# New fixed orders for all five engines of an adaLN block with linear attention and a SiLU MLP, up to the MLP's second unit

## The chip, the cores and the metric

The kernel runs on one core of a Trainium2 chip. A core has five engines, each with an instruction queue of its own that is worked off strictly in order: TensorE (PE in the profile; its weight loads are shown as PEld), VectorE (DVE), ScalarE (ACT), GpSimd (POOL) and SyncE (SP), which here only issues DMAs. Engines wait for each other through semaphores. The metric is the device time of one execution in microseconds, the median of several runs. The kernel before takes 1138.91 us (three runs, 1138.76 to 1139.21).

## The reference

Input x has 2048 tokens of 576 values. A conditioning vector gives six vectors of 576 (shifts, scales and gates). Then come linear attention with 32 heads of 18 values and an MLP with 4608 hidden values, each behind a LayerNorm and each added back with its gate.

```python
mod = (_silu(c) @ w_mod).reshape(c.shape[0], 6, 1, -1)
sa, ca, ga, sb, cb, gb = (mod[:, 0], mod[:, 1], mod[:, 2], mod[:, 3], mod[:, 4], mod[:, 5])
h = _layernorm(x, axis=-1) * (1 + ca) + sa
x = x + ga * _A_ref(h, A_wqkv, A_wo)
h = _layernorm(x, axis=-1) * (1 + cb) + sb
x = x + gb * _B_ref(h, B_w1, B_w2)
...
phi = lambda t: jnp.where(t > 0, t + 1, jnp.exp(t)) + 1e-6
pq, pk = phi(q), phi(k)
kv = jnp.einsum("bhsd,bhse->bhde", pk, v)
z = jnp.einsum("bhsd->bhd", pk)
num = jnp.einsum("bhqd,bhde->bhqe", pq, kv)
den = jnp.einsum("bhqd,bhd->bhq", pq, z)[..., None] + 1e-6
...
h = jnp.einsum("bsd,df->bsf", x, w1)
h = _silu(h)
out = jnp.einsum("bsf,fd->bsd", h, w2)
```

## The kernel before

Nearly all products are made in three passes over operands split into a rounded high part and a remainder (`x_passes`, L226): high by high, high by low, low by high. So most results cost one ACT operation that rounds (a CAST) and one VectorE subtraction that gives the remainder (`sub_hi`, L121).

The 2048 tokens are 16 tiles of 128, in four blocks of 512. The program goes through these stages:

- The head, up to about 36 us. The modulation columns are summed from `w_mod` (L360, L362, matmuls L371), the first block's x is normalised (L191, L193), turned by TensorE transposes (L390) and modulated (L199, L201), and the key product of the first two tiles is made (L407) while its weights are still being loaded and split (L309, L310, L315, L317; L317 on POOL). `warm_up` (L412) gives PE matmuls whose result nobody reads. A one-column exponential, `warm` (L431), stands in the program right behind the SiLU of the conditioning vector.
- The attention's first part, up to about 200 us: for each tile the key, value and query products (`k_proj`, `v_proj`, `q_proj`; matmuls L226 into the two `psK` tiles, two PSUM banks each), the map phi (L326 the exponential on ACT; L333 and L334 on VectorE), the split of v (L544, L548), the sum of k by v in three banks that stay in use (L589), and the transposes of the next block (L214). `mod_piece` (L517, L519) sums other parts of the modulation on VectorE.
- The turn to the second part, up to about 223 us: the product of kv and the output weights (L777).
- The attention's second part and the first piece of the MLP, up to about 368 us, in banks `big` (three of two banks) and `small` (two): transposes of the normalised q (L812), the attention's output (L226), LayerNorm again, the chunks of the second hidden input (`turn_chunk_k`, L214 into `small`), and the first 256 hidden values of the MLP (L886 up with SiLU L888, L897 down).
- The rest: 17 groups of 256 hidden values, each in two units of 1024 tokens (`do_unit`), with matmuls up (L1324) and down (L1397) by seven products in place of eight. From the third unit on, about 402 us, every engine works in the order of the code (`manual_schedule(engines=ENGINES)`).

Up to the second unit a scheduler sets the order of the engines that aren't in a `manual_schedule` block, and the table `ORDERS` overrides it: `arrange` (from L135 on) takes, engine by engine, the instructions in the order in which the code wrote them, numbers them, and ties each to the one before it in the table, without a semaphore wait of its own. Before, PE was in `manual_schedule` too, and its table row was the code's own order but for two transposes; DVE, ACT, POOL and SP had full tables.

```python
tc.add_manual_dep(i, before.name, no_wait, reason="arrange")
```

Of the kernel before, what the change touches and what calls it, by code (L numbers as in the profile page):

```python
# [2 lines left out]

# [19 lines left out]
def kernel(ctx: ExitStack, tc, A_x, A_wqkv, A_wo, B_x, B_w1, B_w2, c, w_mod, out):  # L23
# [28 lines left out]
    def f32(ap):  # L52
# [1 line left out]

    ORDERS = {
        "PE": """
            0-106 114 107-109 115 110-113 116-2586
        """,
        "DVE": """
            0 3 2 1 4 6-7 11 8 12-13 9-10 14-16 18 17 5 19-22 30 23-24 28-29 25-27 43 31 44 33-34 36 35 37-38 32 39  # L60
            41 40 42 45-47 50 48-49 62-63 51-53 57 84 64 55 58 65 59 86 66 85 87 60 56 80 67 88 81 83 68 82 69 71 70
            72 122 73-74 61 89 54 75 78 76 90 77 79 123 91 124 92-93 96-97 125 98 94 126-127 100 99 95 101 103-104
            107 105 108 106 109 111 102 132-133 135 110 134 136 138-139 137 140-144 112 145 148 113 146 149 147 114
            117 115 118 116 119-121 128-129 131 150-151 225 223 130 226 224 222 152-155 157-158 156 159 162 176 160
            177-178 161 179-181 163 165 228 227 166-167 164 169-170 168 171-173 193-197 199 198 200 202 201 203-205
            174 209 206-207 210 208 175 182 185 183 186 188 187 184 189-190 192 191 211-213 216 214 217 215 218 220
            219 221 229 232 230 233 231 234-237 240 238-239 241-243 246 244 247 245 248-249 252 250-251 253-256 258
            257 259 263 260-262 266 268 267 270 269 271 264-265 272-273 275-277 274 281 279 282 278 280 283-284 288
            285 289 286 295-296 290 306 303 302 291 307 292 314 293 315 294 297 323 304 298-299 324 308 331 287 300
            309 301 310-311 305 312 316 332 340 313 317-319 341 320-321 325 351 322 326-329 352 362 330 333-336 338  # L70
            363 337 339 344 370 345-347 342-343 349 348 353 371 380 354-359 350 360 381 361 398 364-369 399 416
            372-375 377 376 378 417 424 385 382 384 379 387-388 391-392 394 425 402 386 389 403 390 404-407 393 383
            395 413 408 412 409 397 418 396 414 410 415 401 419 411 420-421 423 400 422 427-428 426 429 431-439 430
            440 445 441 446 443 442 444 447-451 455 454 453 452 466 456 467 469 457 464 471 458-460 475 472 462 461
            463 478 473 477 484 483 485-486 479 468 480 474 487 470 465 493 488 495 490 476 489 482 492 481 491 494
            529 500-501 499 497 496 498 510 503 502 511 507 506 504-505 508 515 509 514 527 513 512 518 528 519
            516-517 523 520-522 524-526 531 530 533 532 534-535
        """,
        "Activation": """
            0-2 4-6 9 7-8 10 3 11-12 16 19 13-14 18 17 15 21 26 20 27 22-23 29 24 28 25 30-31 35 32-33 36-37 55 57  # L80
            39 56 40 38 42 41 44 43 58 45 50 53 59 54 34 51-52 60 46 48-49 47 61-62 65 63 66-67 69 68 70 64 71-75
            77-78 76 79 81-82 80 83 93 95 94 84-85 96 87 86 88-91 97 92 99 98 100-102 104-105 103 106 108-109 107
            150 149 110-111 151 112 153 152 113-114 116-117 115 118 120 119 121-122 131 133 123-124 132 134 126 125
            127-130 135 137 136 138-139 141-142 140 145 143 146 144 147-148 154-155 157-158 156 159 161 160 162-182
            184 186 185 183 188 187 189-190 193 191 194-195 192 196-198 200 202 199 201 203-208 212 217 209 214 213
            210 216 211 219 215 224 234 220 218 239 221 225 222-223 235 245 228 230 226 232 256 227 231 229 233
            236-237 240 238 241 243 242 246 249 270 247 244 250-251 248 272 252-253 257 254-255 278 266 264 267 265
            258 261 268-269 262 271 263 260 293 259 273 305 274-276 281 283 282 277 284 279 307 285-287 296 289 280
            288 290 292 291 301 299 297 302 306 303 300 304 294-295 308 298 309-311 313 312 314-317 322-323 321 320
            319 318 324 341 325 339 326 342 327 338 344 328 330 340 332 329 333 331 343 347 336 334 337 335 349 345  # L90
            348 353-354 350 355-356 351 358 352 357 346 359 364-365 363 387 360-361 369 371 368 366 362 374 367 370
            372 376 378 373 384 377 379 375 389 385 381-383 386 380 388 390-395 397 396
        """,
        "Pool": """
            6-7 0 3 8 2 4-5 9-15 20 16-17 19 18 21-27 34 28 31 29 35 30 32-33 38 36 42 37 39 45 48 40 43-44 51 46-47
            41 55 49-50 58 52-53 61 56-57 73 85 54 59-60 77 62-63 80 64 74 65 75 68-69 78 66 72 70 79 76 67 71 81-84
            90-92 95 93 86-88 94 101 89 103 105 99-100 96 106 98 121 97 102 107 123-124 104 108-109 114 111 110
            112-113 115-116 118-120 125 122 117 126-128
        """,
        "SP": """  # L100
            0-25 57 30-31 26 28 27 29 32 39 33-34 54 53 55-56 40-46 35-38 47-52 61 63 60 66 64 58 62 65 59 67 69 68
            70-71 75-76 74 72-73 77-82 85 83 86 84 87-88 95 91 89 92 97 93 90 98 94 96 99-102 104 103 119 106-107
            105 110 117 108 118 112 109 111 113-116 123 120-122
        """,
    }

# [531 lines left out]

    QB = NT // 2
    qs = iter(range(NT))  # L640
    with tc.manual_schedule(engines={mybir.EngineType.PE}):
        for t in range(NT):
            tb, i = t // 4, t % 4
            more = tb + 1 < NB
# [43 lines left out]
            if t == 10:  # L688
                load_wo()

    with tc.manual_schedule(engines={mybir.EngineType.PE}):
        qs = iter(range(QB, NT))
        finish_wo()
        edges_of_wo(range(NHC - 2))
# [524 lines left out]
                lns[tb].normalise(i, xn2[tb][i], acc[4 * tb + i], A if tb < 2 or i in (0, 1) else V)  # L1219


    with tc.manual_schedule(engines={mybir.EngineType.PE}):
# [322 lines left out]

    unit = None
    units = [(g, p) for g in range(1, NG) for p in range(2)]
    with tc.manual_schedule(engines={mybir.EngineType.PE}):
        fetch(5)
        for u in U:  # L1550
            G.memset(u, 0.0)
# [41 lines left out]
```

## Time and profile before

| what | value |
|---|---|
| median of three runs | 1138.91 us |
| the profiled execution, span on the core | 1136.9 us |
| instructions in the profile | 19287 |
| HBM read, written | 250.12 MB, 16.78 MB |
| granted TensorE clock, every slice | 0.9 or more |
| mean DMA rate over the span | 237 GB/s |

The profiled execution has no time of its own beside the span; the 2.0 us between the span and the median lie outside of it. A row of the timeline begins with its start in us from the span's start and its duration; neighbours of one line are merged (x4 is four of them), and brackets give the idle time before it and what ended it. A row of the waits gives the total in us, the count and the longest. A row of the windows gives the length of the stretch and the busy time and count of each engine, then the clock, the DMA share and GB/s.

### The profile page before, as it was taken

What the parts mean: (1) busy time and instruction counts of PE and PEld (TensorE: products, weight loads), DVE (VectorE), ACT (ScalarE), POOL (GpSimd) and SP (SyncE); (2) the same over time, 40 slices, a digit from 0 to 9 for tenths busy, and PEclk for the clock granted to TensorE, in tenths of its full rate; (3) what the DMA queues carried; (4) which work ended last, traced back from release to release, by engine and by line L of the source; (5) the groups of instructions that cost most, each with busy time, mean ns of one, the idle gap of its engine ahead of it and who ended that gap; (6) DMA issues with size and microseconds to landing.
All of it is one profiled execution on the core that took longest, in us unless ns stands there. A gap on an engine that the chain in (4) does not pass through costs nothing.

```text
span 1136.9 us, 19287 instructions
## 1 busy us (share of the span) xinstructions
PE 1126.8 (99%) x7033; PEld 1040.8 (92%) x7033; DVE 971.0 (85%) x1543; ACT 538.7 (47%) x1112; POOL 649.3 (57%) x743
## 2 busy tenths in 40 slices
PE   8999999999999999999999999999999999999998
PEld 7999999999998899999999999999989999999998
DVE  6866744686878899999999999999999999999996
ACT  5643442547556544445445444444444444444441
POOL 1100000374714777767775776677667767776786
PEclk9999999999999999999999999999999999999999
DMA  9621100223359877976978869779778697697684
GB/s 281 199 84 31 44 7 1 71 84 116 137 198 354 340 274 256 348 278 257 361 261 315 314 250 356 273 255 364 261 277 331 265 344 281 258 346 274 256 310 156
DMA packets 58813, 269.03 MB, mean 237 GB/s; under 512 B 5724, under 2 KB 21856, under 8 KB 35680
## 3 DMA queue, kind: packets, MB, share of 16 engines
q1 hardware_dynamic: 58708, 267.80, 64.4%
q8 instruction: 56, 0.92, 0.3%
q14 instruction: 37, 0.30, 0.1%
q10 hardware_dynamic: 12, 0.00, 0.0%
HBM read 250.12 MB, written 16.78 MB: 235 GB/s over the span
## 4 chain that ended last, share of the span: by engine, by line
PE 94%; DMA 3%; DVE 1%; ACT 1%; POOL 0%; SPq 0%; issue 0%; POOLq 0%
PE up L1324 34%; PE down L1397 32%; PE psK L226 12%; PE big L226 7%; PE small L886 2%; PE big L897 2%; PE kvp L589 1%; DMA hT<-in_w_mod_dram 1%; PE big L812 1%; DMA raw<-in_w_mod_dram 1%; DMA hT<-hd 1%; PE small L214 1%; DMA xt<-in_A_x_dram 1%; PE up L1427 1%; PE down L1427 1%; PE psT L214 1%
## 5 line engine op out<-in xcount | busy, mean ns | idle before, releaser
L1405 DVE TENSOR_TENSOR acc<-down,acc 128x576 f32<-128x576 f32 x330 | 246.2, 754 | 13.2 <-PE down L1397 3.2
L1324 PE MATMUL up<-hT,w 128*128 128x512 f32 x916 | 239.4, 390 | 0.5 <-DMA hT<-hd 0.5
L1324 PEld LDWEIGHTS up<-hT,w 128*128 128x128 f32 x916 | 164.5, 188 | 25.4 <-DMA hT<-hd 0.7
L1359 POOL TENSOR_TENSOR s<-f,f 128x256 f32<-128x256 f32 x66 | 52.3, 792 | 159.7 <-ACT f L1340 159.7
L1397 PE MATMUL down<-w,hb 128*128 128x288 f32 x792 | 120.6, 294 | 0.0
L1397 PE MATMUL down<-w,hc 128*128 128x288 f32 x792 | 120.6, 294 | 0.0
L1397 PEld LDWEIGHTS down<-w,hc 128*128 128x128 f32 x792 | 113.7, 188 | 5.4 <-PE up L1324 0.3
L1397 PEld LDWEIGHTS down<-w,hb 128*128 128x128 f32 x792 | 113.7, 188 | 5.3
L121 DVE TENSOR_TENSOR w<-v,w 128x288 fp32r<-128x288 f32 (+1 forms) x170 | 114.8, 684 | 2.8 <-ACT w L1058 2.8
L1405 DVE TENSOR_TENSOR U<-down,U 128x576 f32<-128x576 f32 x132 | 99.6, 754 | 17.1 <-PE down L1397 15.2
L226 PE MATMUL psK<-w,hT 128*128 128x352 f32 (+3 forms) x506 | 106.4, 336 | 1.1 <-POOL w L317 0.6
L1324 PE MATMUL up<-room,w 128*128 128x512 f32 x348 | 91.0, 390 | 0.0
L1378 POOL TENSOR_TENSOR hc<-s,hc 128x512 fp32r<-128x512 f32 x66 | 89.4, 1355 | 0.1
L184 POOL TENSOR_TENSOR rstd<-ve,neghalf 128x4 f32<-128x4 f32 (+3 forms) x10 | 9.5, 953 | 138.8 <-DVE ve L183 138.8
L226 PEld LDWEIGHTS psK<-w,hT 128*128 128x128 f32 x506 | 81.8, 188 | 7.5 <-POOL w L317 0.8
L1340 ACT ACTIVATE f<-f 128x512 f32<-128x512 f32 x102 | 64.5, 632 | 47.8 <-DVE f L1345 24.8
L1343 DVE TENSOR_TENSOR f<-up,p 128x512 f32<-128x512 f32 x102 | 69.7, 683 | 12.1 <-PE up L1324 11.2
L1066 ACT CAST w<-v 128x288 fp32r<-128x288 f32 x85 | 36.7, 434 | 76.4 <-PE down L1397 62.1
L1324 PEld LDWEIGHTS up<-room,w 128*128 128x128 f32 x348 | 62.5, 188 | 9.4
L1363 POOL TENSOR_TENSOR f<-f,s 128x256 f32<-128x256 f32 x66 | 51.2, 776 | 34.9 <-DVE hb L1378 24.5
L1397 PE MATMUL down<-w,he 128*128 128x288 f32 x396 | 63.0, 294 | 0.0
L1397 PE MATMUL down<-w,ha 128*128 128x288 f32 x396 | 63.0, 294 | 0.0
(310 smaller groups left out, 2529.7 us busy)
## 6 DMA issues: line engine op xcount, KB each, us to landing
hT<-hd SPq DMA_DIRECT2D x66, 1280.0 KB, 5.5
hT<-hd SPq DMA_DIRECT2D x45, 1024.0 KB, 5.5
room<-hd SPq DMA_DIRECT2D x35, 1280.0 KB, 5.7
room<-hd SPq DMA_DIRECT2D x20, 1024.0 KB, 5.1
v<-in_B_w_dram SPq DMA_DIRECT2D x17, 576.0 KB, 7.2
v<-in_B_w_dram SPq DMA_DIRECT2D x17, 512.0 KB, 7.1
hd<-S SPq DMA_DIRECT2D x6, 1024.0 KB, 3.8
xt<-in_A_x_dram SPq DMA_DIRECT2D x16, 288.0 KB, 5.2
```

The lines of the kernel that those rows point to most:

```text
L121: return V.tensor_sub(lo, full, f32(hi))
L214: T.transpose(ps[:, i * P : (i + 1) * P], xt[i][:, cidx * P : (cidx + 1) * P], ident)
L226: T.matmul(ps, xpart(a), wpart(b), start=n == 0, stop=n == len(XW) - 1)
L1066: A.copy(self.w2[n][:, 0], src)
L1324: T.matmul(ps, left, right, start=first and m == 0, stop=m == len(seq) - 1, skip_group_check=True)
L1340: A.activation(self.f[i, k], self.f[i, k], AF.Silu)
L1343: V.tensor_add(f, self.bank[bank[1]], self.p1)
L1359: G.tensor_add(self.s[:, 0:1], half(i, 0, 1), half(i, 1, 1))
L1363: G.tensor_sub(half(i, 1, 0), half(i, 1, 0), self.s[:, 1:2])
L1378: eng.tensor_sub(t[:, :, 1, :], src, f32(t[:, :, 0, :]))
L1397: T.matmul(ps[:, p, :HALF], self.a[i, n][:, u, p * P : (p + 1) * P], self.w.w2[n][:, v], start=n in (1, 5, 7, 6) and j == 0, stop=j == 2, ...
L1405: V.tensor_add(dst, ps[:, :, :HALF], dst)
```

## The change

The five tables are replaced and the five `manual_schedule(engines={PE})` blocks become plain blocks, so that PE's order comes from its table alone. The numbers in the tables stand for the same instructions as before. Lines after the table are 82 further down in the changed file.

```diff
     ORDERS = {
         "PE": """
-            0-106 114 107-109 115 110-113 116-2586
+            0-3 8 4-5 37 6-7 38 9 39 10-17 19-20 29-36 21-22 72-73 78-79 18 25 23 26 24 40-41 43-45 27 46 42 47 28 48
+            80 54-55 58-59 51-53 66-71 49-50 62 56 63 57 74-75 81 60-61 82 64-65 83 76-77 84-85 88 86-87 90-91 94-95 89
...
-    with tc.manual_schedule(engines={mybir.EngineType.PE}):
+    with nullcontext():
         V.memset(ones, 1.0)
```

What this does is shown at three places, with buffer numbers kept (they differ a little between the programs: `psK_408` of the changed one is `psK_413` of before, `psK_486` is `psK_491`, `psK_580` is `psK_585`).

First, ACT and SP in the head. ACT before, from the end of the first block's modulation on, with the table load of the exponential:

```order
L205 CAST hT_102<-raw_154 128x256
L431 ACT_TABLE_LOAD
L431 ACTIVATE warm_100<-sc_87 128x1
L368 COPY tmod_118<-tmod_118 128x64
L368 COPY hT_117<-hT_117 128x2x64
```

ACT before, some ten rows later: `w_103` is a piece of the value weights, `xt_136` and `xt_138` are the tiles 2 and 3 of x, `e_372` is the exponential of tile 0's keys:

```order
L309 CAST w_103<-acc1_96 128x576
L191 ACTIVATE xt_136<-xt_136,nm_160,rstd_159 128x64
L191 ACTIVATE xt_136<-xt_136,nm_160,rstd_159 128x576
L309 CAST w_103<-acc1_96 128x576
L191 ACTIVATE xt_138<-xt_138,nm_160,rstd_159 128x64
L326 ACTIVATE e_372<-psK_247 128x576
L191 ACTIVATE xt_138<-xt_138,nm_160,rstd_159 128x576
```

ACT after, at the same place; `warm` is now the 121st of ACT's table:

```order
L391 CAST w_103<-acc1_96 128x576 x2
L273 ACTIVATE xt_136<-xt_136,nm_160,rstd_159 128x64
L273 ACTIVATE xt_138<-xt_138,nm_160,rstd_159 128x64
L273 ACTIVATE xt_136<-xt_136,nm_160,rstd_159 128x576
L408 ACT_TABLE_LOAD
L408 ACTIVATE e_370<-psK_245 128x576
L391 CAST v_104<-acc2_97 128x576
L273 ACTIVATE xt_138<-xt_138,nm_160,rstd_159 128x576
```

The table load has moved from behind the first modulation to right ahead of the first exponential. SP before, from its sixth load on (`hT` and `tmod` are pieces of `w_mod`, `acc` holds the raw q, k and v weights):

```order
L230 DMA acc0_95<-in_A_wqkv_dram 128x576 x2
L287 DMA hT_117<-in_w_mod_dram 128x2x320 x2
L285 DMA tmod_118<-in_w_mod_dram 64x320 x2
L287 DMA hT_117<-in_w_mod_dram 128x2x320 x2
L230 DMA acc0_95<-in_A_wqkv_dram 128x576 x2
L232 DMA acc1_96<-in_A_wqkv_dram 64x576
L260 DMA xt_136<-in_A_x_dram 128x576
L260 DMA xt_138<-in_A_x_dram 128x576
L230 DMA acc1_96<-in_A_wqkv_dram 128x576 x3
```

SP after:

```order
L369 DMA hT_117<-in_w_mod_dram 128x2x320 x2
L312 DMA acc0_95<-in_A_wqkv_dram 128x576 x2
L369 DMA hT_117<-in_w_mod_dram 128x2x320
L367 DMA tmod_118<-in_w_mod_dram 64x320
L369 DMA hT_117<-in_w_mod_dram 128x2x320
L367 DMA tmod_118<-in_w_mod_dram 64x320
L314 DMA acc1_96<-in_A_wqkv_dram 64x576
L312 DMA acc0_95<-in_A_wqkv_dram 128x576
L342 DMA xt_136<-in_A_x_dram 128x576
L342 DMA xt_138<-in_A_x_dram 128x576
L312 DMA acc0_95<-in_A_wqkv_dram 128x576
L312 DMA acc1_96<-in_A_wqkv_dram 128x576 x2
```

These loads change places among themselves; the second of the last row's pair, which is the second load of the x3 row before, has the same loads ahead of it in both.

Second, PE at the end of tile 0's value product (`psK_413` before, `psK_408` after). `w_106` is what POOL's L317 writes last, `psT` the transposes of x, `psK_491` the value product of tile 1. Before:

```order
L226 MATMUL psK_413<-v_104,hT_102 128x256
L226 MATMUL psK_413<-v_104,hT_102 128x324
L226 MATMUL psK_413<-w_106,hT_102 128x256
L226 MATMUL psK_413<-w_106,hT_102 128x324
L226 MATMUL psK_413<-w_106,hT_102 128x256
L226 MATMUL psK_413<-w_106,hT_102 128x324
L390 MATMUL psT_448<-ident_85,xt_136 128x128 x2
L390 MATMUL psT_448<-ident_85,xt_138 128x128 x2
L226 MATMUL psK_491<-w_103,hT_102 128x256
L226 MATMUL psK_491<-w_103,hT_102 128x324
```

After:

```order
L308 MATMUL psK_408<-v_104,hT_102 128x324
L308 MATMUL psK_486<-w_103,hT_102 128x256
L308 MATMUL psK_486<-w_103,hT_102 128x324
L308 MATMUL psK_486<-v_104,hT_102 128x256
L308 MATMUL psK_486<-v_104,hT_102 128x324
L308 MATMUL psK_486<-w_103,hT_102 128x256
L308 MATMUL psK_486<-w_103,hT_102 128x324
L308 MATMUL psK_408<-w_106,hT_102 128x256
L308 MATMUL psK_486<-w_103,hT_102 128x256
L308 MATMUL psK_408<-w_106,hT_102 128x324
L308 MATMUL psK_408<-w_106,hT_102 128x256
L308 MATMUL psK_408<-w_106,hT_102 128x324
```

The last four matmuls of tile 0 now have seven of tile 1 ahead of or among them, six of these ahead of the first, and the transposes come later. This is how PE's whole table up to the MLP's first piece reads: two or three products at once, a few matmuls each.

Third, VectorE at the query product of tile 1 (`psK_585` before, `psK_580` after), which L333 has to read before PE can use the bank again. `tmod` is `mod_piece`'s sum. Before:

```order
L193 TENSOR_SCALAR xt_394<-xt_394,mv_459,rstd_461 128x576
L193 TENSOR_SCALAR xt_398<-xt_398,mv_459,rstd_461 128x576
L519 SCALAR_TENSOR_TENSOR tmod_971<-raw_975,sc_87,tmod_971 128x2x576
L333 TENSOR_SCALAR acc0_95<-psK_585 128x576
L519 SCALAR_TENSOR_TENSOR tmod_971<-raw_978,sc_87,tmod_971 128x2x576
L334 SCALAR_TENSOR_TENSOR acc0_95<-e_614,acc0_95 128x576
```

After, with the same L519 (now L601) only 18 rows behind:

```order
L261 BN_AGGR mv_454<-st_466 128x2
L260 BN_STATS st_470<-xt_395 128x6
L261 BN_AGGR mv_454<-st_470 128x2
L265 TENSOR_SCALAR ve_455<-mv_454 128x4
L415 TENSOR_SCALAR acc0_95<-psK_580 128x576
L275 TENSOR_SCALAR xt_389<-xt_389,mv_454,rstd_456 128x64
L267 SCALAR_TENSOR_TENSOR nm_457<-mv_454,rstd_456 128x4
```

L333 (now L415) has moved ahead of the sum of `mod_piece` and ahead of the normalisation of the next block's x.

More of the change, by code (lines that the diff above doesn't have):

```diff
@@ L1 @@
-from contextlib import ExitStack
+from contextlib import ExitStack, nullcontext
 from itertools import count
@@ L58 @@
+            2568-2571 2581 2576 2582-2584 2577-2578 2585 2579 2586
         """,
         "DVE": """
[L60 to L63, printed above, removed]
@@ L74 @@
[L74 to L77, printed above, removed]
+            1 0 10 2 9 6-7 11-12 8 13 18 14 4 19-20 5 15-17 21 24-25 22 29 23 26 28 27 30-31 43 34 33 37 36 35 38 32 39
@@ L640 @@
     qs = iter(range(NT))
-    with tc.manual_schedule(engines={mybir.EngineType.PE}):
+    with nullcontext():
         for t in range(NT):
@@ L689 @@
                 load_wo()
-    with tc.manual_schedule(engines={mybir.EngineType.PE}):
+    with nullcontext():
         qs = iter(range(QB, NT))
@@ L1219, in attn_step @@
                 lns[tb].normalise(i, xn2[tb][i], acc[4 * tb + i], A if tb < 2 or i in (0, 1) else V)
-    with tc.manual_schedule(engines={mybir.EngineType.PE}):
+    with nullcontext():
         for s in range(NT + 2):
@@ L1547 @@
     units = [(g, p) for g in range(1, NG) for p in range(2)]
-    with tc.manual_schedule(engines={mybir.EngineType.PE}):
+    with nullcontext():
         fetch(5)
```

147 lines of the change are left out of this document (117 added, 30 removed).

## The prediction

> **What bounds the kernel now.** I read four views in this order: the page, the busy time by stretch, the waits of TensorE (PE), and the timeline where a wait stands.
>
> ```profile
> span 1136.9 us, 19287 instructions
> ...
> PE 1126.8 (99%) x7033; PEld 1040.8 (92%) x7033; DVE 971.0 (85%) x1543; ACT 538.7 (47%) x1112; POOL 649.3 (57%) x743
> ...
> PE 94%; DMA 3%; DVE 1%; ACT 1%; POOL 0%; SPq 0%; issue 0%; POOLq 0%
> ```
>
> PE is busy for 99% of the span, and the chain that ended last is PE for 94%. No instruction is added or removed, so only time in which PE waits can go. The new orders end at about 402 us; after that the code fixes the order as before. The stretches:
>
> ```profile
> 0.00:36.00 36.00, 31.54 (x215) 29.28 (x216) 25.39 (x64) 23.31 (x46) 8.40 (x16) 1.00 0.85 256
> 36.00:402.00 366.00, 364.00 (x2436) 343.21 (x2435) 261.21 (x474) 184.85 (x354) 112.57 (x116) 1.00 0.37 126
> 402.00:1136.90 734.90, 731.30 (x4386) 668.32 (x4384) 684.36 (x1008) 330.53 (x713) 528.33 (x612) 1.00 0.78 291
> ```
>
> The first number after the length is PE's busy time: 4.5 us idle in the first 36 us, 2.0 us from there to 402. The granted clock is 1.00 in all three, so it is no term of the sum. PE's waits between 36 and 402 us, each with total, count and longest:
>
> ```profile
> PE psK L226 <- DVE acc L333: 0.5, 1, 0.5
> PE psK L777 <- ACT acc L330: 0.4, 2, 0.2
> PE small L214 <- ACT H L199: 0.4, 1, 0.4
> PE small L214 <- ACT sl L888: 0.3, 1, 0.3
> PE small L886 <- ACT sl L888: 0.2, 1, 0.2
> ```
>
> These are 1.8 us in six waits, but each costs more than is listed, since a matmul is drawn longer than the step to the next one:
>
> ```profile
> 213.99 0.43 PE L777 MATMUL psK<-bc_ga,vx 126*128 126x288 f32 x2
> 214.25 0.43 PE L777 MATMUL psK<-raw,vx 126*128 126x288 f32 x2
> 214.51 0.43 PE L777 MATMUL psK<-xt,pk 82*128 82x288 f32 x2
> 215.16 0.54 PE L777 MATMUL psK<-raw,vx 126*128 126x288 f32 x2 [0.22 <-ACT acc L330]
> ```
>
> Pairs start 0.26 us apart; the last comes 0.65 us after the one before it, so it lost 0.39 us where 0.22 is listed. I add 0.2 us to each wait: 1.8 + 6 x 0.2 = **3.0 us** is all that listed waits of this stretch can give back. Gaps too short to be listed may hold up to another 1 us; that is an estimate from the 2.0 us idle against 1.8 listed, again with 0.2 for each of a handful.
>
> **The change part by part.**
>
> *PE's own order.* Before, the pieces of work stand one behind the other; now two or three are mixed, a few matmuls at a time. Does mixing cost or save PE time by itself?
>
> ```profile
> 26.26 0.27 PE L390 MATMUL psT<-ident,xt 128*128 128x128 f32 x1
> 26.28 0.65 PE L407 MATMUL psK<-w,hT 128*128 128x288 f32 x3
> 26.77 0.27 PE L390 MATMUL psT<-ident,xt 128*128 128x128 f32 x1
> ...
> 60.24 0.44 PE psT L214 x4
> 60.68 4.11 PE psK L226 x28
> ```
>
> The first rows are the only mixed place of the timeline, the last two are from the chain: four transposes in a block take 0.44 us, 0.11 each. Mixed in, a transpose and three 288-column matmuls take 26.77 - 26.26 = 0.51 us, which is 0.11 + 3 x 0.13. So mixing costs nothing and gains nothing; I take 0.
>
> *A wait that goes, at 51 us.* The first row of that list, in detail:
>
> ```profile
> 49.31 1.42 DVE L519 SCALAR_TENSOR_TENSOR tmod<-raw,sc,tmod 128x1152 f32<-128x1152 f32 x1 [1.66 <-DMA raw<-in_w_mod_dram]
> ...
> 50.64 0.75 DVE L333 TENSOR_SCALAR acc<-psK 128x576 f32<-128x576 f32 x1
> ...
> 51.45 0.50 PE L226 MATMUL psK<-w,hT 128*128 128x512 f32 x1 [0.48 <-DVE acc L333]
> ```
>
> PE needs the bank that L333 empties. L333 stood on VectorE (DVE) behind a 1.42 us operation that had itself waited for a load. In the new DVE order that L519 stands 18 rows behind L333, and L333 has LayerNorm statistics ahead of it. With the hindrance gone, 0.5 + 0.2 = 0.7 us is saved. What is late next is the same bank's exponential on ACT and L333 itself, 1.4 us together, under about 2 us of mixed PE work.
>
> *The other five.* At 262 us PE turns two pairs of chunks back to back through two `small` banks and waits for ACT's copy out of the first; now `big` matmuls of 0.13 us stand between the transposes, about 1.9 us of PE work from the last transpose of the one chunk to the first of the next but one. That saves 0.4 + 0.2. The waits of `small` on L888 (0.3 and 0.2) go in the same way, 0.9 us with their additions. L777's two matmul groups keep their PE order; ACT has one of the two copies further ahead, so I count one as saved (0.4) and one as kept. The sum is 0.7 + 0.6 + 0.9 + 0.4 = **2.6 us saved**, with ends of 1.5 (only those whose order I can name) and 4.0 (all listed waits and the short gaps).
>
> *The head, up to 36 us.* Here the SyncE queue, ACT and PE are all re-ordered. ACT, before:
>
> ```profile
> 13.92 1.28 ACT L431 ACT_TABLE_LOAD   x1
> 15.21 0.20 ACT L431 ACTIVATE warm<-sc 128x1 f32<-128x1 f32 x1
> ...
> 24.07 0.68 ACT L309 CAST w<-acc 128x576 fp32r<-128x576 f32 x1 [0.45 <-DMA acc<-in_A_wqkv_dram]
> 24.65 1.34 ACT L191 ACTIVATE xt<-xt,nm,rstd 128x64 f32<-128x64 f32 x2
> 25.89 0.66 ACT L309 CAST w<-acc 128x576 fp32r<-128x576 f32 x1
> 26.46 0.44 ACT L191 ACTIVATE xt<-xt,nm,rstd 128x64 f32<-128x64 f32 x1
> 26.80 0.63 ACT L326 ACTIVATE e<-psK 128x576 f32<-128x576 f32 x1
> ```
>
> The table for the exponential was fetched at 13.92 us by the one-column `warm` operation of L431, while ACT had nothing else. In the new order L431 stands far behind, and the 1.28 us load stands right ahead of the first real exponential, `e` of L326. Nothing covers it there. The cast at 24.07 us can't come earlier: it waits for a load, and in the SyncE queue the same 22 loads stand ahead of that one in both orders, only exchanged among themselves. So ACT goes on at 24.65 us with the three pieces of L191 in a row (1.34 us, then 0.44 less the 0.1 by which neighbours overlap), to 26.33; the load, to 27.61; `e` starts 27.62 instead of 26.80. That is 0.8 us late. VectorE's L333 takes another 0.76 us before PE gets the bank, and PE has little else ready:
>
> ```profile
> 27.46 0.76 DVE L333 TENSOR_SCALAR a<-psK 128x576 f32<-128x576 f32 x1
> ...
> 28.24 0.44 PE L390 MATMUL psT<-ident,xt 128*128 128x128 f32 x2 [0.68 <-ACT xt L191]
> 28.43 0.51 PE L226 MATMUL psK<-w,hT 128*128 128x256 f32 x2
> ...
> 32.48 0.81 PE L226 MATMUL psK<-w,hT 128*128 128x256 f32 x4 [0.57 <-POOL w L317]
> ```
>
> The value matmuls that began at 28.43 begin at 27.62 + 0.63 + 0.03 + 0.76 + 0.04 = 29.1, and the two transposes of 28.24 (0.2 us) with one key matmul (0.13) are still to do: 1.0 us lost. Against it, the wait at 32.48 (0.57 + 0.2 = 0.8 us) is covered: six matmuls of the next tile, 0.8 us, now stand ahead of that instruction. Behind it the ACT casts of `wq`, which now stand ahead of the evictions of the first value tile, and are as late as the load, cost an estimated 0.3 us (half of one 0.66 us cast). The head loses 1.0 - 0.8 + 0.3 = **0.5 us**; the ends are a gain of 0.8 (the load is hidden because `e` waits for its matmuls anyway) and a loss of 1.3 (nothing covered).
>
> [...] The trace disagrees as to the drain: 13.92 + 1.28 = 15.20, and the next operation starts at 15.21; I give this 0.03, within "same".
>
> *New waits.* In the new order I counted, for each PE instruction that waits on another engine, the PE work between it and the PE instruction that its chain begins with, against the chain's own durations. About 60 places have under 0.3 us to spare (before: a dozen); behind the head one is short, by 0.6 us in both orders alike. What stands in such a place is late as soon as an operation runs long:
>
> ```profile
> 222.03 1.43 POOL L1196 TENSOR_TENSOR prod<-acc,z 128x576 f32<-128x576 f32 x1
> ...
> 222.54 1.54 DVE L334 SCALAR_TENSOR_TENSOR acc<-e,acc 128x576 f32<-128x576 f32 x1 [4.55 <-ACT acc L331]
> ...
> 383.07 1.32 DVE L1378 TENSOR_TENSOR ha<-f,ha 128x256 fp32r<-128x256 f32 x1
> ...
> 28.25 0.76 DVE L334 SCALAR_TENSOR_TENSOR a<-e,a 128x576 f32<-128x576 f32 x1
> ```
>
> The same L334 takes 0.76 us alone and 1.54 us beside a GpSimd (POOL) operation: 0.8 us more. The two middle rows are the first and the last of some 15 VectorE operations before 402 us that took at least 0.3 us longer than their like. I allow no such hit in the sum's middle and keep 0 to 6 for the range.
>
> **Sum.** The profiled execution spans 1136.9 us, 2.0 us under the 1138.91 us median; what lies around the span is not touched. The change is -2.6 + 0.5 = -2.1 us, so 1134.8 us of span and **1136.8 us**.
>
> **The rivals.**
>
> *A: the sum holds*, 1135.8 to 1137.8 us. For it: the waits are named one by one, and most have a cover in the new order. The PE-bound part behind 402 us carries a shift unchanged, since only one 0.5 us wait stands in it.
>
> *B: nothing is lost in the head, and short gaps go too*: 1138.9 - 3.0 - 0.5 = 1135.4 us, down to 1134.1 with 4.0 saved and the head's end of 0.8. For it: with the trace's own durations the small slacks lie above zero nearly everywhere. Against it: the table load stands uncovered in ACT's rows.
>
> *C: slower.* The price is a VectorE operation held by GpSimd in a tight place, 0.8 us less the 0.25 to spare, 0.55 us each. The profile has some 15 candidates. From 4 hits on the 2.1 us are eaten up, from 8 on the kernel is slower by 0.2%; 8 hits with the head's worst end (0.8 more) give 1136.8 + 4.4 + 0.8 = 1142.0 us. Against it: POOL is idle in most of the first 200 us, and a wait once taken gives all the later chains room. [...]
>
> *D: the gain is given back behind 402 us.* Fetches of `hT` from DRAM run at 291 GB/s, and PE waits for one:
>
> ```profile
> PE up L1324 <- DMA hT<-hd: 0.5, 1, 0.5
> ```
>
> If the transfers and not PE set that stretch, an earlier PE waits longer: 1138.9 us, no change. Against it: it is one wait of 0.5 us in 735.
>
> **How the numbers follow.** A measurement of this kernel can tell about 0.2%, 2.3 us, from no change, so "faster" means under 1136.6 us. A has 0.52 and lies on both sides of that line: 0.22 faster, 0.30 same. B has 0.18, all faster. D, the drain and a small loss have 0.13, same. C has 0.17, slower. Faster is 0.40, same 0.43, slower 0.17. The range leaves out the last tenth on each side: 1134.4 (B with nearly all) to 1140.4 (C with 5 hits and the head's loss of 1.3).
>
> **What would show it.** Right, if in the new profile the table load stands at about 26.3 us with `e` behind it; if the waits on L333 at 51 us and on `H` at 262 us are gone; if PE's idle time from 36 to 402 us is under 1 us; if the first matmul of L1324 comes about 2 us earlier. Wrong, if many waits of 0.1 to 0.5 us on DVE and ACT stand in place of six (C), if the stretch behind 402 us is longer than 734.9 us (D), or if the head ends before 36 us with more done (B).

## The result and the profile after

The changed kernel takes 1150.15 us (median of four runs, 1148.97 to 1152.96). The kernel before took 1139.06 us beside it. The ratio is 1.0096 with an interval of 1.0077 to 1.0116, so the change costs 11 us. The page of the changed kernel, its head, the busy times and the shares of the chain that ended last:

```profile
span 1146.8 us, 19311 instructions
...
PE 1131.0 (99%) x7033; PEld 1041.1 (91%) x7033; DVE 980.5 (85%) x1543; ACT 540.2 (47%) x1112; POOL 649.7 (57%) x743
...
PE 87%; DVE 4%; DMA 4%; ACT 2%; issue 1%; POOL 1%; SPq 0%; ACTq 0%; DVEq 0%; POOLq 0%
```

The same matmuls keep PE busy for 4 us more than before, and DVE is busy for 9.5 us longer with as many instructions. Seven points of the chain have passed from PE to others, three of them to DVE. Busy time by stretch, first of the changed kernel:

```profile
0.00:36.00 36.00, 30.58 (x215) 28.88 (x216) 25.89 (x60) 22.28 (x41) 7.87 (x16) 1.00 0.76 235
36.00:200.00 164.00, 164.00 (x1075) 154.26 (x1073) 101.61 (x201) 70.93 (x141) 6.21 (x8) 1.00 0.20 60
200.00:330.00 130.00, 126.99 (x913) 121.03 (x913) 98.15 (x168) 73.39 (x131) 66.24 (x63) 1.00 0.30 103
330.00:402.00 72.00, 68.62 (x403) 60.95 (x402) 61.11 (x96) 38.67 (x77) 35.57 (x39) 0.98 0.81 290
```

The kernel before in the last three of these stretches:

```profile
36.00:200.00 164.00, 163.42 (x1069) 153.90 (x1068) 101.69 (x199) 69.07 (x138) 5.42 (x8) 1.00 0.19 56
200.00:330.00 130.00, 129.09 (x945) 125.14 (x944) 97.54 (x174) 75.50 (x135) 67.73 (x63) 1.00 0.35 117
330.00:402.00 72.00, 71.50 (x426) 64.18 (x425) 61.97 (x102) 40.29 (x82) 39.41 (x45) 1.00 0.81 302
```

The first number after the length is PE's busy time, the one in brackets behind it its matmuls. Up to 200 us the new orders are a little ahead: no idle time is left. Then PE is idle 3.0 us of 130 and 3.4 us of 72, the granted clock falls to 0.98, and PE does 32 and 23 matmuls fewer in the same time. PE's waits of the changed kernel from 36 to 402 us:

```profile
PE big L979 <- DVE acc L984: 2.0, 1, 2.0
PE big L979 <- ACT hs L971: 1.1, 1, 1.1
PE big L894 <- DVE qT L203: 0.9, 2, 0.7
PE big L979 <- DVE hs L203: 0.7, 2, 0.4
PE psK L308 <- DVE w L397: 0.7, 1, 0.7
PE big L308 <- DVE qT L203: 0.6, 1, 0.6
PE psK L859 <- ACT acc L412: 0.2, 1, 0.2
```

Of the six waits of before only one on L330 (L412 here) is left. In their place stand others on DVE and ACT, and the largest is at 358 us.

To put runs beside each other I use PE's **lateness at equal work**: a matmul's start, less the sum of the steps of all matmuls ahead of it in that kernel, each at its step when nothing waits (0.11 us for a transpose, 0.13 for 288 columns, 0.23 for 512, the medians in the trace of before). The table shows the difference to the kernel before at the same amount of work. It is worked out from one profile of each kernel, and the experiments stand in it too. The profiled execution isn't always a typical one: those of e8, e10 and e12 took 1.5, 2.1 and 2.6 us longer than the medians of their kernels, that of e11 1.6 us less.

| us of PE work | 30 | 50 | 200 | 330 | 350 | 390 |
|---|---|---|---|---|---|---|
| changed kernel | 0.1 | -0.8 | -0.6 | 2.5 | 8.2 | 10.0 |
| e1_first | 0.2 | -0.6 | -0.5 | 0.4 | 0.2 | 0.0 |
| e2_first325 | 1.4 | 0.5 | 0.7 | 5.8 | 6.7 | 6.6 |
| e3_last325 | -0.4 | -0.4 | -0.7 | -1.2 | 6.8 | 8.8 |
| e4_pool | 1.0 | 0.2 | 0.3 | 3.4 | 8.6 | 10.3 |
| e5_act | 0.8 | 0.0 | 0.3 | 3.7 | 9.4 | 11.2 |
| e6_thin | 0.4 | -0.6 | -0.4 | 1.7 | 2.2 | 4.0 |
| e7_thin_before | -0.5 | -1.0 | -1.3 | -1.3 | -0.9 | -0.7 |
| e8_mix1 | 2.4 | 1.7 | 2.2 | 2.9 | 2.9 | 2.9 |
| e9_mix2 | 0.2 | -0.6 | -0.1 | 5.3 | 5.1 | 5.2 |
| e10_local | 0.3 | -0.5 | -0.8 | -1.9 | 1.1 | 1.2 |
| e11_warm | -0.4 | -0.8 | -0.8 | 2.5 | 7.7 | 9.6 |
| e12_local2 | 1.8 | 1.1 | 0.8 | -0.3 | 0.6 | 1.4 |

The changed kernel loses 3.1 us between 200 and 330 us of work, 5.7 in the next 20, and 1.8 in the last 40. The first column shows how far one profile's head can be trusted: e8 and e9 have the same tables up to 27 us of work, and at 20 us of work, ahead of that point, they differ by 2.2 us. Of this 1.7 us is clock. In e8, and in e12 alike, PE ran near half clock from about 24.5 to 28 us (0.57 in the last but two numbers, and 4 x 0.43 = 1.7); the other heads have no such stretch:

```profile
24.00:28.00 4.00, 4.00 (x20) 4.00 (x20) 3.18 (x7) 3.22 (x7) 0.72 (x1) 0.57 1.02 221
```

What happens at 353 us, from the timeline of the changed kernel. The first two rows are two-input operations of DVE while POOL is idle, the next four such operations beside POOL's; then come POOL, PE and ACT:

```profile
358.91 0.69 DVE L203 TENSOR_TENSOR hT<-sl,hT 64x512 fp32r<-64x512 f32 x1
359.63 0.69 DVE L203 TENSOR_TENSOR hT<-S,hT 128x512 fp32r<-128x512 f32 x1
...
355.86 1.76 DVE L203 TENSOR_TENSOR hT<-S,hT 128x512 fp32r<-128x512 f32 x1
...
360.58 1.77 DVE L203 TENSOR_TENSOR hT<-S,hT 128x512 fp32r<-128x512 f32 x1
362.27 3.46 DVE L203 TENSOR_TENSOR S<-S 128x512 fp32r<-128x512 f32 x2
365.66 1.29 DVE L1221 TENSOR_TENSOR S<-S,H 128x512 f32<-128x512 f32 x1
...
351.17 1.38 POOL L1089 TENSOR_TENSOR v<-v,bc_gb 128x288 f32<-128x288 f32 x1 [4.63 <-DMA v<-in_B_w_dram]
...
361.76 1.74 POOL L1242 TENSOR_TENSOR ht<-ht,sl 128x512 f32<-128x512 f32 x1
363.46 1.73 POOL L1222 TENSOR_TENSOR H<-H,S 128x512 f32<-128x512 f32 x1
...
358.34 0.40 PE L979 MATMUL big<-w,hs 128*128 128x288 f32 x1 [1.95 <-DVE acc L984]
...
366.98 0.62 ACT L1166 CAST S<-S 128x512 fp32r<-128x512 f32 x1 [7.45 <-DVE S L1221]
```

The two engines take turns: an operation of POOL ends at 354.24 us, one of DVE at 354.78, then POOL's at 355.38, DVE's at 355.93, POOL's at 357.07 and DVE's at 357.62. DVE's operation takes 1.76 us where its like takes 0.69, beside POOL operations of 1.7. From 353 to 367 us DVE is busy without a gap (13.94 of 14 us), and eight of its operations are 7.2 us longer in all than their like. PE waits for L984, which stands behind them. ACT waits 7.45 us for the last of them, with the SiLU that PE needs queued behind that wait, so that PE waits once more:

```profile
369.48 2.72 PE L979 MATMUL big<-w,hs 128*128 128x288 f32 x18 [1.11 <-ACT hs L971]
```

### The profile page after: what moved, and what is told of

It reads as the page before. It is cut to its first block, busy times and chain, and to the rows that moved or that the text cites. A ratio compares the mean times of both kernels' runs of the same rounds, so it can differ in the third digit from the quotient of the medians.

```text
span 1146.8 us, 19311 instructions
## 1 busy us (share of the span) xinstructions
PE 1131.0 (99%) x7033; PEld 1041.1 (91%) x7033; DVE 980.5 (85%) x1543; ACT 540.2 (47%) x1112; POOL 649.7 (57%) x743
## 4 chain that ended last, share of the span: by engine, by line
PE 87%; DVE 4%; DMA 4%; ACT 2%; issue 1%; POOL 1%; SPq 0%; ACTq 0%; DVEq 0%; POOLq 0%
PE up L1406 33%; PE down L1479 31%; PE psK L308 13%; PE big L308 4%; PE kvp L671 1%; DVE hT L203 1%; PE big L979 1%; DMA acc<-in_A_wqkv_dram 1%; DMA v<-in_B_w_dram 1%; DMA hT<-hd 1%; PE psT L296 1%; PE up L1509 1%; PE down L1509 1%; DMA xt<-in_A_x_dram 1%; PE big L894 0%
## 5 line engine op out<-in xcount | busy, mean ns | idle before, releaser
L1487 DVE TENSOR_TENSOR acc<-down,acc 128x576 f32<-128x576 f32 x330 | 245.8, 753 | 13.0 <-PE down L1479 4.0
L1406 PE MATMUL up<-hT,w 128*128 128x512 f32 x916 | 242.5, 390 | 0.4 <-DMA hT<-hd 0.4
L308 PE MATMUL psK<-w,hT 128*128 128x288 f32 (+4 forms) x506 | 117.7, 343 | 2.2 <-DVE a L415 1.7
L1487 DVE TENSOR_TENSOR U<-down,U 128x576 f32<-128x576 f32 x132 | 99.5, 754 | 17.8 <-PE down L1479 15.8
L308 PE MATMUL big<-w,qT 128*128 128x288 f32 x352 | 70.0, 307 | 0.6 <-DVE qT L203 0.6
L1479 PE MATMUL down<-w,hd 128*128 128x288 f32 x396 | 63.9, 294 | 0.0
```

The source lines that it names most:

```text
L308: T.matmul(ps, xpart(a), wpart(b), start=n == 0, stop=n == len(XW) - 1)
L1406: T.matmul(ps, left, right, start=first and m == 0, stop=m == len(seq) - 1, skip_group_check=True)
L1479: T.matmul(ps[:, p, :HALF], self.a[i, n][:, u, p * P : (p + 1) * P], self.w.w2[n][:, v], start=n in (1, 5, 7, 6) and j == 0, stop=j == 2, ...
L1487: V.tensor_add(dst, ps[:, :, :HALF], dst)
```

## The experiments

Theory L said that the loss arises late, behind 200 us, and theory H that it arises there by DVE operations that POOL holds. Its rivals: a loss spread over all tight places (S), one late load in POOL's queue (P), ACT's order (A), or orders too tight in themselves (O).

**Which part of the tables loses.** Three kernels take the new tables up to a point and the old ones behind it, or the reverse. On POOL, e2's table differs from the changed kernel's like this (numbers are POOL's instructions), the other engines' in the same manner:

```diff
-            81-84 90-91 100 86 92 87 93 88 94 89 101 103 105-107 96 102 95 98 104 121 108-109 99 110-111 113 112 123
-            114 124 97 115-116 118 120 119 125 117 126-127 122 128
+            81-84 90-92 95 93 86-88 94 101 89 103 105 99-100 96 106 98 121 97 102 107 123-124 104 108-109 114 111 110
+            112-113 115-116 118-120 125 122 117 126-128
```

> The new tables of all five engines as far as they had got when TensorE had done 205 us of work (1359 matmuls, about 218 us in the trace of the changed kernel), the old tables behind that point. Theory L (the loss arises late, behind 200 us): the head and the removed 51-us wait are kept, so 0.6 us less than the kernel before up to 0.2 more: 1138.3 to 1139.3 us. Theory S (the tight places are everywhere, a loss spread evenly over the 402 us): about half of the 11 us, 1144 us.

> The new tables as far as 325 us of TensorE work (2246 matmuls, about 346 us in the trace of the changed kernel), the old tables behind that point. Theory L as the offset between the two traces has it (2.5 us late at 330 us of work, 6.9 at 340, 10 at 390): 1141 to 1142.5 us. If the stretch before only sets up a late collision, whichever tables stand behind it: 1146 or more. Theory S: 1148.

> The old tables as far as 325 us of TensorE work, the new ones behind. Theory L: the last 60 us of the new tables lose 7 us on their own, 1145.5 to 1147 us. If they lose only because the stretch before has left VectorE behind: 1139 to 1140 us. Theory S: 1141 us.

Measured: e1 1139.77 us (ratio 1.0014, 0.9999 to 1.0030), e2 1145.96 (1.0061, 1.0039 to 1.0082), e3 1148.51 (1.0077, 1.0053 to 1.0101). S is out: the new tables up to 205 us of work cost next to nothing, though not 0.6 us less either. Behind 325 us they lose 10 us on their own (e3, by the table -1.2 to 8.8), more than the 7 expected. e2 missed its number by 4 us and lies where its rival said (1146 or more, if the stretch before only sets up a late collision). Its trace doesn't bear that rival out: at 325 us of work e2 is 4.9 us late already, and only 1.7 us are added behind. 1.4 us is its head, and the change of tables at 325 us brings waits of its own, 1.5 us on the SiLU among them.

**One move on POOL.** The row above shows POOL waiting 4.63 us for its load, with the sums behind it.

```diff
-            81-84 90-91 100 86 92 87 93 88 94 89 101 103 105-107 96 102 95 98 104 121 108-109 99 110-111 113 112 123
+            81-84 90-91 86 92 87 93 88 94 89 100-101 103 105-107 96 102 95 98 104 121 108-109 99 110-111 113 112 123
```

> The changed kernel with one instruction moved: POOL's first product with the gate (L1089, which waits 4.63 us for its load and stands ahead of the sums L1219 to L1222) goes behind those sums. Theory P (this wait pushes the sums into VectorE's densest stretch, where the two hold each other up, and that costs the 4.3 + 1.3 us between 330 and 350 us of TensorE work): 1145 to 1146.5 us, and the two-input VectorE operations there take 0.7 us again. Theory V (VectorE's own order is too tight there and would be late anyway): 1149 us or more.

Measured: 1149.00 us (1.0082, 1.0058 to 1.0105). P falls, and the profile of e4 shows why:

```profile
361.36 3.48 DVE L203 TENSOR_TENSOR S<-S 128x512 fp32r<-128x512 f32 x2
...
366.08 0.62 ACT L1166 CAST S<-S 128x512 fp32r<-128x512 f32 x1 [7.47 <-DVE S L1221]
...
368.58 3.61 PE L979 MATMUL big<-w,hs 128*128 128x288 f32 x15 [2.70 <-ACT hs L971]
```

The wait on L984 fell from 2.0 to 0.4 us, but the held pair is still there, and the loss came back ten microseconds later as a wait on `hs`.

**Two moves on ACT.**

```diff
-            336-337 331 335 347-348 350 353 345 349 354 343 355-356 340 352 351 357 338 358 346 359 363-365 360-361 369
+            336-337 331 335 347-348 353-354 350 345 349 343 355-356 340 352 351 357 338 358 346 359 363-365 360-361 369
```

> The changed kernel with two ACT instructions moved: the SiLU of the MLP's first up product (sl L970) and its rounding (hs L971) go ahead of the cast S L1166 that waits 7.45 us for VectorE's L1221. Theory A (ACT's order holds the SiLU back, and TensorE's wait on hs at 368 us goes with it, 1.3 us listed, about 2 with the lower clock behind it): 1147 to 1148.5 us. Theory D (VectorE is full there, so that the remainder of hs, which stands behind L1221 on VectorE, is late in any case): 1149.5 to 1150.5, with the wait now on VectorE's L203.

Measured: 1149.96 us (1.0089, 1.0072 to 1.0106). D holds. PE's two largest waits in e5 are now both on DVE:

```profile
PE big L979 <- DVE acc L984: 2.7, 2, 2.0
...
PE big L979 <- DVE hs L203: 1.1, 2, 0.6
```

**Shorter POOL operations, same orders.**

```diff
         def sums(c, eng):
-
-            t0, t2 = rows[c], rows[2 + c]
-            eng.tensor_sub(h32s[:, c], h32s[:, c], t0)
+            m = slice(0, 64 if eng is G else 512)
+            t0, t2 = rows[c][:, m], rows[2 + c][:, m]
+            eng.tensor_sub(h32s[:, c, m], h32s[:, c, m], t0)
...
-        G.tensor_sub(tail32, tail32, t)
+        G.tensor_sub(tail32[:, :64], tail32[:, :64], t[:, :64])
```

> The changed kernel with POOL's sums of the second hidden input (L1219 to L1222 and L1242, eleven operations of 512 columns) cut to 64 columns; the orders and the number of instructions are the same, and the sums of the other 448 columns are left out where POOL makes them. Theory H (VectorE's two-input operations are held by these POOL operations, and that makes VectorE late at 320 us and from 353 to 367): those VectorE operations take 0.7 us again, the waits of L979 on L984 and hs go, and the time is 1142 to 1144.5 us. Theory O (the orders themselves are too tight, or the late load is what counts): 1147.5 us or more.

> A control: the old tables with POOL's sums cut in the same way. If the cut acts only through the time for which POOL holds VectorE, little is to be gained here, since TensorE waits 1.8 us in all behind 36 us: 1137.8 to 1139 us under both theories. If it is under 1137, the cut saves something of its own, and e6 has to be read against that.

(There are fourteen such operations, not eleven.) Measured: e6 1142.97 us (1.0035, 1.0024 to 1.0046), e7 1138.09 (0.9989, 0.9974 to 1.0004). H holds: by the ratios some 7 of the 11 us go. The old tables gain 0.4 us by the medians from the same cut (1.3 by the ratio, whose interval ends at 3.0), so most of the gain belongs to the new orders. By the table 5.2 us of it are saved between 330 and 350 us of work, where e6 loses 0.5 us and the changed kernel 5.7. In e6:

```profile
357.47 0.81 DVE L203 TENSOR_TENSOR hT<-S,hT 128x512 fp32r<-128x512 f32 x1
358.21 1.54 DVE L203 TENSOR_TENSOR S<-S 128x512 fp32r<-128x512 f32 x2
...
363.54 2.69 PE L979 MATMUL big<-w,hs 128*128 128x288 f32 x18
```

DVE's operations are back at 0.7 to 0.8 us (the x2 row is two of them), and the down matmuls at 363 us start without a wait. The cut also makes POOL's results ready sooner. In the changed kernel ACT waited for three of these sums, 1.8, 1.4 and 0.3 us, but PE's waits from 353 to 368 us run over DVE (L984, and ACT's 7.45 us on L1221), and DVE waited for none of these sums there, so little of the gain can be that. What is left in e6 (4 us by the table) are waits outside these sums: on qT at 229 us (1.0 us lost), on `w` L397 at 216 (0.8), on `hs` at 288 (0.7), on qT at 255 (0.4), and 0.6 on L1487 at 399.

**The head.** `warm` goes back to where ACT is idle.

```diff
-            0-2 4-8 10 9 11 21 12 16 13-14 17 15 18-20 26-27 22 24 23 28 30 25 29 32 31 33 59 55 35 37 57 39 58 40-41
...
-            112-114 118-119 116-117 122 115 3 120-121 123-124 126-127 125 133 150 128-129 131 134 132 137 135 130 136
+            0-8 10 9 11 21 12 16 13-14 17 15 18-20 26-27 22 24 23 28 30 25 29 32 31 33 59 55 35 37 57 39 58 40-41 56 42
...
+            118-119 116-117 122 115 120-121 123-124 126-127 125 133 150 128-129 131 134 132 137 135 130 136 149 141-142
```

> The changed kernel with the one-column exponential (warm) put back early on ACT, behind the SiLU of the conditioning vector, where ACT is idle for 5 us. Theory T (the table load ahead of the first exponential is what TensorE waits for at 26 us): the wait of 1.75 us on L415 falls to about 0.5, and 1.2 us are saved, 1148.8 us. Theory C (the head is late for other reasons, so the exponential waits for its matmuls or for the normalised x anyway): the wait stays above 1.3 us and the time within 0.5 us of 1150.

The changed kernel's timeline at this place, and then e11's row of the same matmul:

```profile
25.25 1.28 ACT L408 ACT_TABLE_LOAD   x1
26.55 0.65 ACT L408 ACTIVATE e<-psK 128x576 f32<-128x576 f32 x1
...
28.04 0.54 PE L308 MATMUL psK<-w,hT 128*128 128x256 f32 x2 [1.75 <-DVE a L415]
```

```profile
27.58 0.54 PE L308 MATMUL psK<-w,hT 128*128 128x256 f32 x2 [0.26 <-DVE a L415]
```

Measured: 1149.47 us (1.0095, 1.0072 to 1.0119). The wait falls by 1.5 us, so T holds as to the mechanism. PE reached this place 1.0 us later in e11 than in the changed kernel, though, so the fairer partner is e5, which has the late `warm` and reached it at the same time as e11 (the last matmul ahead starts at 26.95 and 26.94 us):

```profile
28.79 0.53 PE L308 MATMUL psK<-w,hT 128*128 128x256 f32 x2 [1.47 <-DVE a L415]
```

Against that row e11 begins 1.2 us earlier, which is what T expected. In the medians it is 0.7 us, within what the runs scatter.

**Can the better places be put into the old tables?** First whole stretches. The old SP table changes like this in both, the other engines' in the same manner:

```diff
-            0-25 57 30-31 26 28 27 29 32 39 33-34 54 53 55-56 40-46 35-38 47-52 61 63 60 66 64 58 62 65 59 67 69 68
+            0-25 57 30-31 26 28 27 29 32 39 33-34 40-41 54 42-43 53 56 35-37 44 55 45 38 46-52 63 61 64 66 58 60 67 59
```

> The old tables up to 27 us of TensorE work (the head), the new ones from there to 205 us, the old ones behind. If the removed waits are worth what the prediction gave them (0.7 us at 51 us, 0.3 near 130) and nothing new is lost on this stretch: 1.0 us less than the kernel before, 1137.5 to 1138 us. If the head's part of the new tables was what gained, or the seam costs a wait: 1138.5 to 1139.5 us.

> As e8_mix1, with the new tables also from 239 to 256 us of TensorE work, where the wait of small on H at 261 us stands. If that wait (0.6 us) goes and the seams cost nothing: 0.6 us under e8_mix1, 1136.9 to 1137.4 us. If the new tables bring their own wait on qT at 255 us into this stretch (0.4 us): 0.2 us under e8_mix1.

Measured: e8 1139.35 us (1.0006, 0.9990 to 1.0022), e9 1143.89 (1.0043, 1.0027 to 1.0059). Neither gains what was hoped for. The wait at 51 us goes in both (0.8 us by the table), and in e9 the one at 261 too (0.7). But the first seam (the place where the tables change), at 27 us of work, costs both 0.9 us, and the wait on L397 at 216 us comes with the new tables. Behind the seam at 256 us of work, inside the pipelined stretch, e9 loses 5 us within the next 25 us of work, with new waits of 1.8 us on `hs` and 0.8 on hT among them, and 1.7 us by half clock behind the first of these (granted clock 0.998 over the execution).

Then single moves, three of them (PE's row, and on DVE number 123, the waiting L519; the rows break at other places):

```diff
-            0-106 114 107-109 115 110-113 116-2586
+            0-106 114 107-109 115 110-113 116-1658 1665-1672 1659-1664 1673-2265 2270-2275 2266-2269 2276-2586
...
-            72 122 73-74 61 89 54 75 78 76 90 77 79 123 91 124 92-93 96-97 125 98 94 126-127 100 99 95 101 103-104
+            122 73-74 61 89 54 75 78 76 90 77 79 91 123-124 92-93 96-97 125 98 94 126-127 100 99 95 101 103-104 107 105
```

> The old tables with three local moves. VectorE: the L519 that waits for its load at 49 us goes behind the L333 that TensorE waits for (0.64 us lost at 51 us). TensorE: the two chunks of transposes at 260 us go six matmuls earlier, so that work stands ahead of the third chunk (0.60 us lost at 261 us), and six L979 matmuls go ahead of the transposes at 347 us (0.41 us). If the waits are worth what the trace shows and nothing takes their place: 1.6 us less than the kernel before, 1136.8 to 1137.4 us. If what is late next takes their place (ACT behind L333, the qT cast, the next bank): 1138 to 1139 us.

Measured: 1137.63 us (0.9999, 0.9983 to 1.0014). All three waits are gone: by the table 0.3 becomes -0.5 at 50 us of work, and -1.9 is reached at 330. Then, in the profiled execution, 3.0 us are lost at once, at a place where the old tables had no wait:

```profile
358.45 4.96 POOL L1089 TENSOR_TENSOR v<-v,bc_gb 128x288 f32<-128x288 f32 x1 [5.12 <-DMA v<-in_B_w_dram]
...
358.65 0.67 DVE L203 TENSOR_TENSOR hs<-sl,hs 128x512 fp32r<-128x512 f32 x1
...
362.00 0.74 DVE L203 TENSOR_TENSOR w<-raw,w 128x256 fp32r<-128x256 f32 x2
...
367.27 1.85 PE L979 MATMUL big<-w,hs 128*128 128x288 f32 x12 [2.76 <-DVE acc L984]
```

The same L1089 (L1007 before) took 0.82 us in the kernel before:

```profile
358.64 0.82 POOL L1007 TENSOR_TENSOR v<-v,bc_gb 128x288 f32<-128x288 f32 x1 [4.08 <-DMA v<-in_B_w_dram]
```

In e10 it met DVE's two-input operations, which follow each other without a gap from 358.65 to 362.74 us, and it ended 0.7 us behind the last of them. The sum L1222 stood behind it. As this execution was 2.1 us over the median, not every execution need lose as much. L1222 was moved ahead of L1089 (this diff is against e10):

```diff
-            95 93 86-88 94 101 89 103 105 99-100 96 106 98 121 97 102 107 123-124 104 108-109 114 111 110 112-113
+            95 93 86-88 94 89 101 103 105 99-100 96 106 98 121 97 102 107 123-124 104 108-109 114 111 110 112-113
```

> e10_local with one more move: on POOL the last sum L1222 goes ahead of the first product with the gate L1089, which took 4.96 us there beside VectorE's unbroken run of two-input operations and held L1222 back, and with it ACT, VectorE and TensorE (2.9 us at 364 us). Theory G (L1089 was starved by VectorE because it landed in that run, and only L1222's place behind it cost TensorE anything): the wait at 364 us goes, the three removed waits stay removed, 1136.2 us, 1.6 under the kernel before. Theory N (L1222 is starved in the same way wherever it stands, or another wait comes in its place): 1137.5 to 1139 us.

```profile
360.33 0.81 POOL L1089 TENSOR_TENSOR v<-v,bc_gb 128x288 f32<-128x288 f32 x1 [3.75 <-DMA v<-in_B_w_dram]
```

Measured: 1137.32 us (0.9994, 0.9982 to 1.0006). L1089 takes 0.81 us again and the wait at 364 us is gone, but two smaller ones have come (0.7 us on `hs` at 361, 0.9 on a fetch of `w` at 375). From 30 to 390 us of work e12 gains 0.5 us (1.8 to 1.4 in the table). This profile is 2.6 us over the median of e12, 1.7 of it the half clock in its head (granted clock 0.998 over the execution). N is nearer, and no version here beats the kernel before by more than can be measured.

## Why the prediction was wrong

- *Mixing costs nothing.* Right. Between 50 and 200 us of work, with PE's pieces mixed all along, the lateness changes by 0.2 us.
- *The removed waits, 2.6 us.* Right in the main, place by place. At 51 us 0.8 was gained (0.7 predicted), and e10 gains the same by moving the one DVE operation named. But this wait isn't in every execution: e7, with the old order there, loses 0.2 us and not 0.6, since its load had landed earlier (L519 begins at 48.32 us, 49.31 before). At 262 us the gain was 0.6 (0.6), at the two waits on the SiLU 0.8 (0.9). One wait on L330 stayed, and of the other 0.15 us went (0.4 predicted); a new one on L397 stands beside it.
- *The head, 0.5 us lost.* The sum came near, the parts not all. The table load stands ahead of `e`, at 25.25 us rather than 26.3, since the cast that waits for the load of the weights came earlier; e11 against e5 shows that it costs PE 1.2 us there (1.0 predicted). But the gain set against it didn't come: the wait on POOL's L317 went, yet with a wait on L397 in its place (0.4 us listed) PE loses 0.8 us from 20 to 25 us of work, as in the kernel before. The net shows only over many profiles. At 20 us of work, ahead of every seam, six heads with the new tables (all but e11's) are 0.0 to 1.4 us late, 0.6 on average; seven with the old ones are -0.7 to 1.8, and -0.7 to 0.3, -0.2 on average, without the 1.7 us of half clock in e8 and e12. So the head loses about 0.8 us. The drain that stands among the chances is shown by no run: here too the next operation follows the table load at once, 25.25 + 1.28 = 26.53 and `e` starts at 26.55.
- *New waits, "no such hit in the sum's middle", 0 to 6 for the range.* **This is the step that failed**, and with it rival C's price of 0.55 us per hit. The places were counted, and the VectorE operation held by GpSimd (1.54 us for 0.76) was named in C, with a chance of 0.17. But each hit was priced as one operation against 0.25 us to spare, and the worst case named, 1142.0 us, lies 8 us under the measured time. In the changed kernel's profile the new waits come to some 12 us where the sum has 0: it is 10.0 us late at 390 us of work although 2.3 us of the old waits are gone.

Between 200 and 330 us that price is about right. PE loses 0.8, 0.7, 0.4, 0.7 and 0.8 us at 216, 229, 255, 288 and 320 us, and three of the five are POOL holding DVE: beside a POOL operation DVE's took 1.12 us for 0.15 at 253.85 us, 0.87 for 0.15 at 287.44, and 1.28 for 0.30 at 316.89. The place at 255, in the changed kernel:

```profile
253.85 1.12 DVE L267 SCALAR_TENSOR_TENSOR nm<-mv,rstd 128x4 f32<-128x4 f32 x1 [1.14 <-POOL rstd L266]
...
253.78 1.17 POOL L835 TENSOR_TENSOR pn<-acc,r 128x576 f32<-128x576 f32 x1
```

An operation on four columns, 0.15 us alone, lasts until POOL's is over, and the qT behind it is late. At 229 us it is ACT instead, whose cast waits 2.8 us for a load.

From 353 to 367 us the price was wrong. DVE has no gap in which to catch up (13.94 of 14 us busy), so the excess of eight held operations adds up to 7.2 us. PE lost 5.7 us between 330 and 350 us of work, by two waits of 2.0 and 1.1 us and by the clock (below). That the excess alone doesn't decide is seen between 200 and 330 us: eleven operations of DVE take at least 0.3 us longer than their like there, 7.7 us in all, and PE loses 3.1 us, of which POOL's part is the three places above. By these two stretches a hit is worth 0.55 us only on an engine that is idle soon afterwards. I had the sign of that in the trace of before, where DVE was busy for 7.96 of 8 us from 362 us on (the third busy time), and did not look at how dense DVE was around the tight places:

```profile
362.00:370.00 8.00, 8.00 (x54) 7.47 (x54) 7.96 (x14) 4.03 (x9) 3.08 (x4) 1.00 0.95 359
```

- *"POOL is idle in most of the first 200 us"*, which spoke against C, was true, and from 36 to 200 us no DVE operation takes 0.3 us longer than its like. The loss came where POOL's sums stand.
- *D, given back behind 402 us.* Ruled out as predicted: 10.0 us late at 390 us of work, 9.9 at the end of the span.

Still open is why the new orders bring POOL's five sums of the last block into that stretch. In the kernel before they began 345.49 to 359.42 us, in the changed one 352.51 to 363.46. The late load explains the first only (e4). L1220 and L1221 wait for remainders on DVE (2.97 and 2.26 us in e4), so DVE's own order is the likely cause; moving those remainders ahead was not tried.

## What to carry to other kernels

Waits that are named in a profile can be removed, and at their own place they give what they show; but e10 and e12 removed three without a gain that could be measured, since others came in their stead. In a pipeline with 99% on one engine the question is where the other engines get late next. Before an order is made tighter, look for stretches where a second engine has no gap at all: there every delay adds up instead of being caught up, as the 7.2 us did here. Two engines that take turns, as DVE (1.76 us for 0.69) and POOL did here, count as one engine there, and a shift of under a microsecond can decide which of them is held (L1089 began 1.8 us behind the start of DVE's three L984 in e10 and took 4.96 us; 1.1 us behind in e12, and took 0.81).

## What the hardware showed that I had not expected

- **Starving the other way.** Beside DVE's unbroken two-input operations a POOL operation of 0.82 us took 4.96 us (e10). In the changed kernel the two alternate, 1.76 us for DVE's operation and 1.7 for POOL's. Cut to an eighth (e6), four of POOL's five sums still took 0.77 us at this place, where six of the same took 0.32 or 0.33 elsewhere: by estimate from these two, the drawn duration holds a wait of some 0.45 us. In e10 POOL's operation lost to eight DVE operations in a row, which cost it 4.1 us. What decides between alternating and losing was not shown.
- **Half clock after a wait of 2 us, and what it cost.** After PE's wait of 1.95 us the changed kernel shows this clock (last but two numbers):

```profile
356.00:358.00 2.00, 0.38 (x3) 0.05 (x1) 2.00 (x2) 1.39 (x3) 2.00 (x2) 1.00 0.89 338
358.00:360.00 2.00, 1.66 (x8) 1.57 (x9) 1.94 (x4) 0.62 (x1) 0.20 (x1) 0.82 0.62 255
360.00:362.00 2.00, 2.00 (x7) 1.73 (x7) 2.00 (x3) 0.00 (x0) 1.53 (x2) 0.50 0.20 62
362.00:364.00 2.00, 2.00 (x10) 1.67 (x8) 2.00 (x3) 0.00 (x0) 2.00 (x2) 0.82 0.75 251
```

and e11 after the same wait, of 2.0 us, this one:

```profile
358.00:360.00 2.00, 2.00 (x13) 1.83 (x13) 1.94 (x4) 0.62 (x1) 0.06 (x1) 1.00 0.44 183
360.00:362.00 2.00, 2.00 (x12) 1.72 (x11) 2.00 (x3) 0.00 (x0) 2.00 (x2) 1.00 0.36 90
```

The clock falls short of 1.00 by 1.7 us of PE time (2 x 0.18 + 2 x 0.50 + 2 x 0.18), which is some 3.4 us at half clock. Between 330 and 340 us of work the changed kernel fell back by 4.3 us and e11 by 2.2, with the same wait. The wait alone doesn't decide whether it comes: of four profiles with a wait of 2.0 us at this place, the changed kernel and e5 have the half clock (granted clock 0.999 over the execution in both), e3 and e11 don't (1.00 from 354 to 366 us). But little of it was lost in the end, because DVE set the pace. Where the changed kernel waits 1.11 us for `hs` afterwards, e11 arrives earlier and waits longer:

```profile
368.97 6.74 PE L979 MATMUL big<-w,hs 128*128 128x288 f32 x48 [2.72 <-ACT hs L971]
```

From 330 to 350 us of work the two lose 5.7 and 5.2 us.
